# An attention kernel whose written-out engine order begins earlier, with another load order

## The chip, the cores and the metric

The kernel runs on one core of one Trainium2 chip. Its five engines run their own instruction queues in order and meet only through semaphores: TensorE (PE, matrix products into PSUM), VectorE (DVE), ScalarE (ACT), GpSimd (POOL) and SyncE (SP, which here issues DMA transfers). The metric is the device time of one execution in microseconds (us), the median of the runs shown.

## The reference

There are 2048 tokens (S) of width 512 (D), 32 query heads of width 16 (Dh), one key head and one value head that all query heads share, and an MLP of inner width 1792. Cut to what is computed:

```
x  = A_x                                    # 2048 x 512, bfloat16
xn = (x - mean) / sqrt(var + 1e-5)          # layer norm over each token's 512
q  = xn @ wq  -> 32 heads x 16;  k = xn @ wk;  v = xn @ wv        # one k, one v
p  = softmax(q k^T / 4)                     # 32 heads x 2048 x 2048, no mask
s  = concat_heads(p v) @ wo
g  = silu( silu(xn @ w1) @ w2 )
out = x + s * g
```

## The kernel before

**Tiles.** Tokens are cut in 16 tiles of 128 and in 4 chunks of 512 (four tiles each). A chunk serves twice, as 512 queries and as four key tiles. The heads are taken in four octets; of an octet the four even heads make one group and the four odd heads the next, so there are 4 chunks x 4 octets x 2 = 32 head groups. In a head group, the score block of one head with one key tile is a slot (128 keys x 512 queries): 32 x 4 heads x 16 key tiles = 2048 slots.

**PE's two modes.** A score matmul (L1068) uses 32 rows of the array, one head in each strip of 32 rows. Up to four of them, with different strips and each with its own PSUM bank, run side by side: a *score group*. A group that holds a second, *late* score for a strip in use is a *double group*. All else goes by *rounds*, four matmuls side by side that each fill 32 columns: PV (probabilities times values, L1494), the products h (with w1), z (with w2), q and w (with wo) at L696, and the keys K (L743). A *column run* is the rounds between two score groups. Tokens are turned (features to partitions) by PE transposes, eight to a pair of tiles (L712); values V are small matmuls at L773. A round of a product may instead be cut into four *gap pieces* (L808), each of which goes in a row strip that a score group leaves unused. There are seven PSUM banks for scores and products, and bank 7 gathers the PV output of one head group.

**Two ways to an exponential.** An *A slot* is read from PSUM by ACT, which writes exp to `pa_sb` (L1941, one, two or three banks in one instruction) and gives one PV matmul. A *D slot* is evicted by DVE as integers (`db_sb`, L1204, *score eviction*) that read as bfloat16 are a rough exp; POOL adds three constants to them, four slots at a time (int64 add into `ds_sb`, L1414, *shift*), and the four versions are PV matmuls with differently weighted values, whose sum is a better exp. Four D slots so cost four evictions, three shifts and 16 PV matmuls. DVE can do a shift too, but does none here. After a head group DVE transposes the PV output and divides by the softmax's sum (steps a to d, L1550 on).

**The other work on DVE and ACT.** Norms on DVE: statistics of a tile (L607), their aggregate (L611), eight small *root steps* for 1/sqrt, a chain, for four tiles at once (L625 to L634), and the normalised tile (L639). For chunk 0 ACT takes part. The turned tokens of a pair of tiles are copied from PSUM by DVE (L725). Keys are evicted at L757 and values at L782, queries at L818. Silu takes a tanh on ACT (L860, `t_sb`) and a product on DVE (L862, the *gate*). Keys for the odd heads lie 16 partitions further: a DMA that POOL issues copies them (`kt_sb`, L1573, *key copy*), once per chunk. While there are no other instructions, PE multiplies zeros (`zer_sb`): in full width ahead of the first tokens (L1878), in half width by rounds later (the *zero fills*, at L696 by the shared helper `col4`).

**Memory.** The D path's shift buffers `ds_sb` number eight; the last four hold the four chunks of x until their tiles are normalised. Loads go through SP's queue: four single tiles of chunk 0, the small weights and wq, then chunks 1, 2 and 3 of x, then w1 (1.75 MB), w2 (1.75 MB) and wo.

**What sets the order.** Class `Planner` lays out all instructions before the program is built: `place` puts an instruction at the end of an engine's list, `add` hands in a `Task` with a priority and a gate, and `best` picks for an engine the ready task of the lowest priority number. The main loop advances the engine whose planned clock is lowest. The prologue's jobs (turns T, keys K and values V of chunks 0 to 3, `NPRO` of them) and everything around them are placed by such rules: `pe_step` for PE, `act_step`, `generic_step`. From a certain state on the strings in `ORDER` dictate what each engine takes next:

```
at["on"] = st["pro"] >= NPRO and not active and x_free[0] and not any(pl.tasks[e] for e in (AC, DV, PO)) and (
    pl.clk[PE] <= min(pl.clk[e] for e in (AC, DV, PO)))
```

So in the kernel before the table begins when keys, values and turns of all four chunks are done. In PE's string, `S21+4B.` is a score group of two A and one D slot (the codes give bank, head group and strip; the last character is a gap piece's strip or a dot), `L` a late score, `Paads-` a PV round with the kind of each strip (a: from `pa_sb`, d: `db_sb`, s: `ds_sb`), `N5` starts the next job in bank 5, `J` is one more round of the active job. ACT's string has the banks per exp and T for a tanh, DVE's string digits (score eviction of that bank) and H (gate), Q (queries), a to d, V and W (outputs), POOL's string only 0 (the first shift in waiting). When the strings end, the rules take over again: last halves of PV, output products with wo of the last chunk, their sums with x, and stores.

Two rules hold before the table: `want_d` allows D slots only when the keys of all 16 tiles have been evicted, and shift buffers 4 to 7 come free together, when all 16 tiles are normalised (`check_x_free`, `make_shifts`).

## Time and profile before

| | |
|---|---|
| median of 3 runs | 657.98 us (657.75 to 658.15) |
| the profiled execution's own time | 658.13 us |
| its span in the trace | 656.3 us |
| granted TensorE clock | 1.00 |
| PE busy | 646.6 us (99%), 9007 matmuls |
| ACT busy | 642.2 us (98%), 748 instructions |
| DVE busy | 614.7 us (94%), 1094 |
| POOL busy | 585.0 us (89%), 583 |
| DMA | 12.86 MB, 20 GB/s on average |
| largest groups | shifts 577.0 us (567), exp 604.4 us (651), score evictions 481.3 us (756) |

The span is what the profiler saw of one execution; the device time lies a little above. Busy is the time in which at least one of an engine's instructions runs. PE's matmuls overlap, four of a group or round run side by side, and their ends are modelled, so the sums of PE's groups exceed its busy time and a busy PE need not be PE at its best; what one step of PE costs is read from the start of one to the start of the next. In rows of the order of time the columns are the start, the time from the first start to the last end of the instructions in the row, engine, line, operation, output and inputs, shape, and the count of like instructions in a row, with a bracket where the engine stood idle before it: for how long, and what released it. In rows of groups, "busy, mean" is followed by the idle time ahead of the group and the engine that ended most of it.

### The profile page before, as it was taken

The page shows a single profiled execution, that of the slowest core. Times are in us where ns is not written, and L with a number is a line of the kernel's source. Part 1 is how long each engine was busy: PE and PEld are TensorE (multiplying, and loading weights), DVE is VectorE, ACT ScalarE, POOL GpSimd, SP SyncE. Part 2 cuts the span into 40 slices and gives each one's busy share as a digit, 9 for nine tenths or more (in the row PEclk, how much of TensorE's full clock was granted, in tenths as well). Part 3 has the DMA queues.
Part 4 walks back from the last instruction along what each step waited for, and adds up shares of the span by engine and source line. Part 5 has one row for each costly group of instructions (what it writes and reads, how often), then busy time and mean ns, then how long its engine had stood idle before and what let it go on. Part 6 is the DMA issues. An engine that isn't in the chain of part 4 may idle for free.

```text
span 656.3 us, 21267 instructions
## 1 busy us (share of the span) xinstructions
PE 646.6 (99%) x9007; PEld 199.4 (30%) x9007; DVE 614.7 (94%) x1094; ACT 642.2 (98%) x748; POOL 585.0 (89%) x583
## 2 busy tenths in 40 slices
...
PEclk9999999999999999999999999999999999999999
...
DMA packets 11501, 12.86 MB, mean 20 GB/s; under 512 B 1808, under 2 KB 10768, under 8 KB 11408
## 3 DMA queue, kind: packets, MB, share of 16 engines
...
q0 software_dynamic: 192, 0.46, 0.2%
q10 hardware_dynamic: 432, 0.39, 0.2%
q14 instruction: 21, 0.17, 0.1%
...
## 4 chain that ended last, share of the span: by engine, by line
PE 92%; POOL 3%; DVE 3%; DMA 1%; ACT 1%; SPq 0%; issue 0%; DVEq 0%
PE ps L1494 42%; PE ps L1068 30%; PE ps L696 19%; POOL ds_sb L1414 3%; DMA ds_sb<-in_A_x_dram 1%; DVE stats_sb L607 1%; ACT pa_sb L1941 1%; PE ps L712 0%; SPq L542 0%; DVE xn_sb L639 0%; DVE kt_sb L757 0%; DVE u_sb L862 0%; DVE xnT_sb L725 0%; DVE v_sb L782 0%; PE ps L743 0%
## 5 line engine op out<-in xcount | busy, mean ns | idle before, releaser
L1414 POOL INT64_ADD ds_sb<-db_sb x567 | 577.0, 1040 | 33.9 <-DVE otr_sb L1554 19.0
L1941 ACT ACTIVATE pa_sb<-ps 128x1024 bf16<-128x1024 f32 (+2 forms) x651 | 604.4, 1040 | 2.7 <-PE ps L1068 2.2
L1204 DVE TENSOR_SCALAR db_sb<-ps 128x512 uint16<-128x512 f32 x756 | 481.3, 682 | 23.4 <-PE ps L1068 12.7
L1494 PE MATMUL ps<-ds_sb,v_sb 128*32 128x512 bf16 x2268 | 287.8, 383 | 0.0
L1068 PE MATMUL ps<-qt_sb,kt_sb 32*128 32x512 bf16 x2048 | 246.1, 384 | 3.4 <-ACT pa_sb L1941 1.3
L1494 PE MATMUL ps<-pa_sb,v_sb 128*32 128x512 bf16 x1296 | 246.4, 383 | 0.0
L1494 PE MATMUL ps<-db_sb,v_sb 128*32 128x512 bf16 x756 | 185.6, 383 | 0.0
L1068 PEld LDWEIGHTS ps<-qt_sb,kt_sb 32*128 32x128 bf16 x2048 | 64.3, 90 | 252.5 <-ACT pa_sb L1941 155.4
L1494 PEld LDWEIGHTS ps<-ds_sb,v_sb 128*32 128x32 bf16 x2268 | 71.6, 95 | 68.4 <-issue 48.9
L1494 PEld LDWEIGHTS ps<-pa_sb,v_sb 128*32 128x32 bf16 x1296 | 60.6, 95 | 38.7 <-issue 28.1
L696 PE MATMUL ps<-xnT_sb,w_sb 128*32 128x512 bf16 x876 | 62.9, 382 | 0.0
L696 PE MATMUL ps<-w_sb,u_sb 128*32 128x512 bf16 x796 | 60.4, 383 | 0.0
L1494 PEld LDWEIGHTS ps<-db_sb,v_sb 128*32 128x32 bf16 x756 | 45.9, 95 | 22.8 <-issue 15.2
L860 ACT ACTIVATE t_sb<-ps 128x512 bf16<-128x512 f32 x72 | 44.8, 622 | 1.7 <-PE ps L696 1.7
L862 DVE SCALAR_TENSOR_TENSOR u_sb<-t_sb,ps 128x512 bf16<-128x512 bf16 x56 | 38.0, 678 | 1.3 <-ACT t_sb L860 0.9
L808 PE MATMUL ps<-w_sb,u_sb 32*128 32x512 bf16 x100 | 38.5, 384 | 0.0
L696 PEld LDWEIGHTS ps<-xnT_sb,w_sb 128*32 128x32 bf16 x876 | 19.1, 95 | 23.4 <-DVE db_sb L1204 6.0
L1573 POOL DMA_DIRECT2D kt_sb<-kt_sb x4 | 2.3, 566 | 24.7 <-DVE kt_sb L757 14.7
L696 PEld LDWEIGHTS ps<-w_sb,u_sb 128*32 128x32 bf16 x796 | 15.7, 95 | 22.2 <-issue 15.0
L1550 DVE STREAM_TRANSPOSE f_sb<-ps 128x512 f32<-128x512 f32 x31 | 21.9, 707 | 0.2
L696 PE MATMUL ps<-wo_sb,on_sb 128*32 128x512 bf16 x256 | 18.6, 382 | 0.0
L696 PE MATMUL ps<-xnT_sb,wq_sb 128*32 128x512 bf16 x228 | 17.0, 382 | 0.0
...
## 6 DMA issues: line engine op xcount, KB each, us to landing
...
xr_sb<-in_A_x_dram SPq DMA_DIRECT2D x16, 128.0 KB, 2.3
out_dram<-ob_sb SPq DMA_DIRECT2D x15, 128.0 KB, 1.7
...
ds_sb<-in_A_x_dram SPq DMA_DIRECT2D x2, 128.0 KB, 2.7
```

The lines of the kernel that those rows point to most:

```text
L607: ts_ = pl.add(Task(DV, 593.0, lambda v, t=t: v.bn_stats(stats_sb[:, t, :], x_tile(t)), [xkey(t)], [("st", t)], 1 + j, gate=(lambda j=j: S ...
L696: last = h.matmul(bank(b)[32 * j:32 * (j + 1), 0:n], lhsT=lhs(j), rhs=rhs, start=start, stop=stop, tile_position=(0, 32 * j), skip_group_c ...
L808: return (lambda pe: pe.matmul(bank(b), lhsT=lhs(k, rows, 0, P), rhs=rhs(k, rows), start=False, stop=last, tile_position=(32 * i, 0), skip ...
L860: t1 = Task(AC, 490.0, lambda a: a.activation(t_sb[:, k, :], src, ACT.Tanh, scale=scale), [held], [("t", k)], 0, [t0])
L862: t2 = Task(DV, T_P, lambda v: v.scalar_tensor_tensor(out=dst, in0=t_sb[:, k, :], scalar=1.0, in1=src, op0=ALU.add, op1=ALU.mult), [held, ...
L1068: return pe.matmul(bank(b), lhsT=kt_sb[32 * i:32 * i + 32, g % 2, kt * P:(kt + 1) * P], rhs=qt_sb[32 * i:32 * i + 32, (g // 2) % NQR, :], ...
L1204: bt.P[i] = pl.add(Task(DV, T_P, lambda v: v.tensor_scalar(db_sb[:, bt.b, i * NQ:(i + 1) * NQ], bank(b), 128.0 * LOG2E, 128.0 * (SHIFT_BET ...
L1414: whole["po"].append(pl.add(Task(PO, T_P64, lambda g, cols=cols: g.int64_add(ds_sb[:, s, cols].bitcast(U64), db_sb[:, bt.b, cols].bitcast( ...
L1494: h = pe.matmul(bank(OB)[32 * i:32 * (i + 1), cols], lhsT=lhs, rhs=rhs, start=s0, stop=s1, tile_position=(0, 32 * i), skip_group_check=True)
L1550: t1 = pl.add(Task(DV, T_TR, lambda v: v.transpose(f_sb[:, k, :], bank(OB)), [("ps", OB)], [("F", k)], 1, [norm.get(("m", g - 2))]))
L1573: kt1[c] = pl.add(Task(PO, T_SWDGE, lambda e: e.dma_start(kt_sb[DH:P, 1, cols], kt_sb[0:P - DH, 0, cols]), [("kt0", k) for k in range(4 * ...
L1941: op = pl.place(AC, 0.8333 * NQ * n + T_AF, lambda a: a.activation(pa_sb[:, s * NQ:(s + n) * NQ].rearrange("p (b n) -> p b n", n=NQ), ps3[ ...
```

## The change

- `ORDER` begins earlier: after the prologue jobs of chunk 0 (`N0` of them) have started, the first octet's queries and the keys of chunk 0 are placed and no job but V of chunk 0 is active. All four strings are new. The turns, keys and values of chunks 1 to 3 stand in PE's string as prologue jobs (`M` starts one; `J`, `K`, `L` are rounds of the first, second and third active job). The norms of chunks 1 to 3 stand in DVE's string: s statistics, g aggregate, r root step, x normalised tile, C turned-token copy, E keys, v values; h is a shift done by DVE. In POOL's string 0 is a shift, k a key copy, and y a point up to which POOL waits, in the plan, for one more DVE instruction that the code marks `ports=2`.
- `want_d` asks for four key tiles (`D_TILES`) in place of 16, and a shift buffer that holds a chunk of x comes free when that chunk's four tiles are normalised.
- Loads: chunk 1, first half of w1 (inner columns 0 to 895), chunk 2, chunk 3, second half of w1, w2, wo. The h products wait for their half of w1 alone.
- `keep_warm` puts half-width zero products in the planned gaps of PE within a window of the plan; they replace the zero fills of that stretch, for PE's rules no longer decide there.
- `turn` (tokens turned by DMA transposes) and the normalised tile on POOL exist in the code, but with `T_DMA = 4` and `XN_PO = 4` all 16 tiles are turned by PE and normalised by DVE.
- In the planner, a key copy's landing, loads' durations, and priorities of the norms have other values, and `finish` now marks an output product as done also when its last part was a gap piece.

The strings differ from the old ones all along, up to the last PV. In the changed file the lines lie lower: L747 products and fills, L763 turns, K L802, V L833, gap pieces L869, scores L1134, PV L1563, score evictions L1273, shifts L1484 (POOL) and L1477 (DVE), exp L2011, tanh L921, gate L923, statistics L625, normalised tile L663, turned-token copies L776, key evictions L816, queries L879, key copies L1642.

```diff
@@ -19,6 +19,9 @@
+WARM_END, START_US = 45000.0, 10.0
+T_KT1, X_KB, W1_KB = 3300.0, 700, 1200
+XN_PO, T_DMA, T_XN, D_TILES, AHEAD_PA = 4, 4, 1200.0, 4, 14
...
     PE: (
-        "S216CM.LdfPaaaaN0JS11Yu.LaNJJPaaaaS214Al.LdyPaddaS21N[,.PdaaaPssadS214Bk.N6JJJS21M[..PaassS21:Dm.PssssPssaaPa-ssS01-.S21"
...
+        "JS31Xgt+.JN2JJJS30+4M.N4JJJN5S30+Br.JS207M.PaaadJM0S20Bv.JS209R.LaGM4N0JJJS408Ely.PaaaaM3JJJM0S308E_.S40;Dkx.JM4PaaaaM1S"
+        "30Cfs.PaaaaN0JJS21CLZ.JS306gu.M4JJJPaadaS30*@M.M1JS21hu(.PaaaaS21@NY.M1M0S11is.LaXPaaaaS305BO.PddaaM0JJJS21Yhr.PasasPsss"
...
     AC: (
-        "1122222T22222T2T222221T2T22222222222T2T12222222322T221T222222T2T2222222322222222222222T22323232222222222222T222222212222"
...
+        "33T21111111T13T222122122121222113222222222T222T212222222222T2T3222T2T22T232222222222222T2T2T2232222221T122222222222T2311"
...
     DV: (
-        "356Q56050H506a262bHc6H54656156H1H45645645645646a6H1H5Q25265265b6c5d252H5465H6256256a5Hb6cH2623623635625625625656a56b5c6d"
...
+        "gsg0gvrrrrrrrrHxxxxssssggggQrCrHrCrrrrHrssssxxxxggggErvrCrCr4rQrrrxxxxEv04CC6E62363v62323252H5a264H16456456456456b5c5H65"
+        "H6232a3H5Hb1c4H1d236Q32632632632632636Ha6H6H3b2c32562626126H2652626a4b6c46d46H6154Q636326526524a343b4c343H34040630630630"
...
     PO: (
-        "000000000000000000000000000000000000000000000000000000000000000000000000000000000000000000000000000000000000000000000000"
...
+        "kkkyyyyyyyyyyyy000k0000000000000000000y000000000y00000000000000000000y00000000000000y0000000000000000000y000000000000000"
...
-        for j in range(1, 4):
+        H1 = P * (NFT // 2)
+        w1v = B_w1.rearrange("(dc p) f -> p dc f", p=P)
+
+        def load_x(j):
             dma(SP, "x", ds_sb[:, XB + j, :].bitcast(BF16).rearrange("p (t d) -> p t d", d=D),
-                xv[:, 4 * j:4 * j + 4, :], 512, ds_keys(XB + j), prio=1)
-        dma(SP, "w1", w1_sb[:], B_w1.rearrange("(dc p) f -> p dc f", p=P), 1792, ["w1"], prio=2)
-        dma(SP, "w2", w2_sb[:], B_w2.rearrange("(ft p) n -> p ft n", p=P), 1792, ["w2"], prio=3)
-        dma(SP, "wo", wo_sb[:], A_wo.rearrange("(o p) n -> p o n", p=P), 512, ["wo"], prio=4)
+                xv[:, 4 * j:4 * j + 4, :], X_KB if j == 1 else 360, ds_keys(XB + j), prio=1)
+
+        def load_w1(h):
+            dma(SP, "w1", w1_sb[:, :, h * H1:(h + 1) * H1], w1v[:, :, h * H1:(h + 1) * H1], 600, [("w1", h)], prio=1)
+        load_x(1)
+        load_w1(0)
+        load_x(2)
+        load_x(3)
+        load_w1(1)
+        for name, dst, src, kb in (("w2", w2_sb[:], B_w2.rearrange("(ft p) n -> p ft n", p=P), 1792),
+                                   ("wo", wo_sb[:], A_wo.rearrange("(o p) n -> p o n", p=P), 512)):
+            dma(SP, name, dst, src, kb, [name], prio=4).gate = lambda: T_DMA >= NC or len(turned) == 4 * (NC - T_DMA)
...
                 ts_ = pl.add(Task(DV, 593.0, lambda v, t=t: v.bn_stats(stats_sb[:, t, :], x_tile(t)),
-                                  [xkey(t)], [("st", t)], 1 + j,
-                                  gate=(lambda j=j: STG(j, xn_task, evac_kt)) if j > 1 else
+                                  [xkey(t)], [("st", t)], 1 + j if j < 1 else 0,
+                                  gate=(lambda j=j: (rs_task[j - 1].op if j > 2 else xn_task[7].op) is not None) if j > 1 else
                                   (lambda: ("xnT", 3) in pl.lastw) if j > 0 else None))
-                pl.add(Task(DV, 66.0, lambda v, t=t: v.bn_aggr(mv_sb[:, t, :], stats_sb[:, t, :]),
-                            [("st", t)], [("mv", t)], 1 + j, [ts_]))
+                ts_.tag = "s"
+                ag = pl.add(Task(DV, 66.0, lambda v, t=t: v.bn_aggr(mv_sb[:, t, :], stats_sb[:, t, :]),
...
-                xn_task[i] = pl.add(Task(DV, 323.0, lambda v, i=i: v.tensor_scalar(
+                xn_task[i] = pl.add(Task(DV if g < XN_PO else PO, 323.0 if g < XN_PO else T_XN, lambda v, i=i: v.tensor_scalar(
                     xn_sb[:, i % 4, :], x_tile(i), mv_sb[:, i, 0:1], rstd_sb[:, i:i + 1],
                     op0=ALU.subtract, op1=ALU.mult),
-                    [xkey(i), ("rs", a), ("mv", i)], [("xn", i % 4)], 1 + g, [t], ports=2,
+                    [xkey(i), ("rs", a), ("mv", i)], [("xn", i % 4)], 1 + g if g < 1 else -1, [t], ports=2,
                     gate=lambda i=i: i < 4 or i - 4 in t_done))
+                xn_task[i].tag = "x"
...
+        def keep_warm(extra):
+            pe = list(pl.order[PE])
+            for k, a in enumerate(pe[:-8]):
+                if a.t0 > WARM_END or a.mode not in ("C", "S") or a.t0 < START_US * 1000.0:
+                    continue
+                room = pe[k + 1].t0 - a.end - (0.0 if pe[k + 1].mode == a.mode else SWITCH) - 40.0
+                n = int(room / (MM / 2))
+                c = next((j for j in range(k + 1, k + 5) if pe[j].fresh), None)
+                if n < 1 or c is None:
+                    continue
+                bs = [b for b, (_, ds) in pe[c].fresh.items() if all(pl.vis(d, PE) <= a.end for d in ds) and not any(
+                    b in o.banks for o in pe[k + 1:c])]
+                if not bs:
+                    continue
+                b = bs[0]
+                i, ds = pe[c].fresh[b]
+                if a.mode == "C":
+                    emit = lambda pe, b=b: col4(pe, b, lambda j: zer_sb[:, 32 * j:32 * (j + 1)], zer_sb[:, 0:NQ // 2], True, True, NQ // 2)
+                else:
+                    emit = lambda pe, b=b, r=slice(32 * i, 32 * i + 32): pe.matmul(
+                        bank(b)[:, 0:NQ // 2], lhsT=zer_sb[r, 0:P], rhs=zer_sb[r, 0:NQ // 2], start=True, stop=True, tile_position=(r.start, 0))
+                for _ in range(n):
+                    a = extra(PE, emit, ds, a)
...
+        def turn(t):
...
+            pl.add(Task(SP, 1200.0, lambda e: e.dma_start_transpose(out=xnT_sb[:, :, t * P:(t + 1) * P], in_=xn_sb[:, t % 4, :]),
+                        [("xn", t % 4)], [("xnT", t)], 1, [xn_task[t]], placed, dma=2))
...
-                    lambda k, rows: xnT_sb[rows, k, c * NQ:(c + 1) * NQ], lambda k: ["w1"] + xnT_keys(c))
+                    lambda k, rows: xnT_sb[rows, k, c * NQ:(c + 1) * NQ], lambda k: [("w1", ft // (NFT // 2))] + xnT_keys(c))
...
+        N0 = len(jobs)
         for c in range(1, NC):
-            mk_T([4 * c, 4 * c + 1])
-            mk_T([4 * c + 2, 4 * c + 3])
+            if c < T_DMA:
+                mk_T([4 * c, 4 * c + 1])
+                mk_T([4 * c + 2, 4 * c + 3])
+            else:
+                for t in range(4 * c, 4 * c + 4):
+                    turn(t)
             mk_K(c, 4 * c, 4 * c + 4)
...
-            if any(k not in evac_kt or evac_kt[k].op is None for k in range(NKT)):
+            if any(k not in evac_kt or evac_kt[k].op is None for k in range(D_TILES)):
...
-                    free = [k for k in range(NDS) if ds_busy[k] == 0 and (k < XB or x_free[0])]
+                    free = [k for k in range(NDS) if ds_busy[k] == 0 and (k < XB or all(xn_task[4 * (k - XB) + r].op is not None for r in range(4)))]
...
                 x_free[0] = True
-                make_shifts()
...
-        at = dict.fromkeys((PE, AC, DV, PO), 0) if ORDER else None
+        at = dict.fromkeys((PE, AC, DV, PO, "n", "two"), 0) if ORDER else None
+
+        def started():
+            return st["pro"] >= N0 and all(t is not None and t.op is not None for t in (q_done.get(0), evac_kt.get(3))) and all(
+                jb.kind == "V" for jb in active)
 
         def ordered():
             if not at.get("on"):
-                at["on"] = st["pro"] >= NPRO and not active and x_free[0] and not any(pl.tasks[e] for e in (AC, DV, PO)) and (
-                    pl.clk[PE] <= min(pl.clk[e] for e in (AC, DV, PO)))
+                at["on"] = started() and pl.clk[PE] <= min(pl.clk[e] for e in (AC, DV, PO))
             return at["on"]
 
...
-            if c == "N":
-                jb, b = jobs[st["job"]], int(next_of(PE, 2)[1])
-                if b not in pool_free or jb.gate is not None and not jb.gate() or any(k not in pl.lastw for k in jb.rounds[0][1]):
+            if c in "NM":
+                jb, b = jobs[st["job" if c == "N" else "pro"]], int(next_of(PE, 2)[1])
+                if b not in pool_free or any(p.op is None for p in jb.preds) or jb.gate is not None and not jb.gate() or any(
+                        k not in pl.lastw for k in jb.rounds[0][1]):
                     return INF
-                st["job"] += 1
+                st["job" if c == "N" else "pro"] += 1
                 pool_free.remove(b)
                 jb.bank = b
                 active.append(jb)
                 at[PE] += 1
-            jb = next(jb for jb in active if jb.left and jb.pos < jb.end - (1 if jb.got else 0))
+            else:
+                jb = [jb for jb in active if jb.left and jb.pos < jb.end - (1 if jb.got else 0)]["JKL".index(c)]
             if any(k not in pl.lastw for k in jb.rounds[jb.pos][1]):
-                assert c != "N"
+                assert c not in "NM"
                 return INF
             at[PE] += 1
             do_job(max(pl.clk[PE], pl.ready(PE, jb.rounds[jb.pos][1], [("ps", jb.bank)] if jb.pos == 0 else ())), jb)
...
-            task = next((x for x in pl.tasks[e] if x.tag == tag), None)
+            task = next((x for x in pl.tasks[e] if x.tag == tag and (tag != "h" or pl.avail(x) is not None)), None)
...
+            if e == PO and c == "y":
+                if at["n"] >= at["two"]:
+                    return INF
+                at["n"] += 1
+                at[e] += 1
+                return True
+            if e == PO and c.isdigit():
+                ts = [x for x in pl.tasks[PO] if x.tag is None]
+                if len(ts) <= int(c) or pl.avail(ts[int(c)], False) is None:
                     return INF
                 at[e] += 1
-                pl.place_task(pl.tasks[PO][int(c)])
+                pl.place_task(ts[int(c)])
```

261 lines of the change are left out of this document (141 added, 120 removed).

## The prediction

> **What bounds the kernel now.** I read the page's first two parts, then busy time by stretch, the waits of TensorE (PE) and VectorE (DVE), and the order of time for prices.
>
> ```profile
> span 656.3 us, 21267 instructions
> PE 646.6 (99%) x9007; PEld 199.4 (30%) x9007; DVE 614.7 (94%) x1094; ACT 642.2 (98%) x748; POOL 585.0 (89%) x583
> PEclk9999999999999999999999999999999999999999
> ```
> ```profile
> 8.90:36.60 27.70, 24.39 (x417) 11.36 (x405) 25.39 (x77) 25.72 (x37) 2.77 (x5) 1.00 0.60 207
> 36.60:60.00 23.40, 23.33 (x313) 7.43 (x313) 22.75 (x39) 23.40 (x31) 19.09 (x19) 1.00 0.02 6
> 60.00:640.00 580.00, 579.15 (x8003) 171.64 (x7995) 552.56 (x930) 579.03 (x658) 550.63 (x542) 1.00 0.03 8
> 10.00:20.00 10.00, 8.24 (x146) 4.15 (x146) 9.65 (x34) 8.88 (x9) 0.68 (x1) 1.00 1.06 380
> ```
> Columns of the second fence: stretch, its length, then busy time and count of PE, weight load, DVE, ScalarE (ACT), POOL, the granted clock, DMA share, GB/s. From 60 to 640 us PE and ACT are busy throughout; DVE and POOL have some 5% left. Up to 36.6 us POOL does almost nothing, while DVE is busy 25.39 of 27.70 us. In the waits (total, times, longest) PE stood 0.7 us from 60 to 640, its only such row, and DVE waited 1.4 us for PE once in the first stretch:
>
> ```profile
> PE ps L1068 <- DVE u_sb L862: 0.7, 1, 0.7
> DVE kt_sb L757 <- PE ps L743: 1.4, 1, 1.4
> ```
> So PE's own work sets the middle, and the start is a race of DVE, ACT and PE. Prices of PE, from start to start:
>
> ```profile
> 42.02 0.39 PE L1068 MATMUL ps<-qt_sb,kt_sb 32*128 32x512 bf16 x3
> 42.35 0.39 PE L1494 MATMUL ps<-pa_sb,v_sb 128*32 128x512 bf16 x2
> 42.68 0.39 PE L1068 MATMUL ps<-qt_sb,kt_sb 32*128 32x512 bf16 x3
> ...
> 643.45 3.19 PE L696 MATMUL ps<-w_sb,u_sb 128*32 128x512 bf16 x56
> 646.47 1.04 PE L1494 MATMUL ps<-ds_sb,v_sb 128*32 128x512 bf16 x16
> ```
> A score group takes 0.33, a column run of one round 0.33, and 14 rounds of z 3.02. So: 0.325 a group, 0.216 a round, and 0.115 for each turn back from column to score mode.
>
> **The change, part by part: PE's work.** The two programs' instruction orders can be counted from the first score group to the last output product.
>
> ```
>                    groups (double)  column runs  rounds  turns and V   sum
> before, all        616 (4)          613          1630.0  5.3 us        629.0
> after,  all        613 (4)          608          1629.0  5.3 us        627.2
> before, to K of 3   15               13            32.5  4.8            18.2
> after,  to K of 3   17 (1)           14            36.0  4.7            19.8
> ```
> (0.325, 0.216 for the second half of a double group, 0.115, 0.216.) "K of 3" is the key projection of the last chunk. The rounds leave out zero fills: 60 matmuls of half width before (1.6 us), 12 after (0.3). The fall of 1.8 us has 12 PV matmuls less in it (0.65): 4 slots go from DVE to ACT, 752 of 756 stay, and 8 gap pieces of 132 become two rounds, which puts back 0.4.
>
> ```profile
> 9.94 0.39 PE L1068 MATMUL ps<-qt_sb,kt_sb 32*128 32x512 bf16 x3
> 33.74 1.04 PE L743 MATMUL ps<-xnT_sb,wke_sb 128*32 128x512 bf16 x16
> 36.17 0.39 PE L1068 MATMUL ps<-qt_sb,kt_sb 32*128 32x512 bf16 x3 [0.58 <-DVE u_sb L862]
> 651.34 0.39 PE L1754 MATMUL ps<-xr_sb,ident 128*128 128x512 bf16 x1
> ```
> The profiled run needs 23.8 us from 9.94 to the K of 3 for 18.2 us of work: 5.6 lost, 1.6 of them as fills. From there 33.74 + (629.0 - 18.2) = 644.5, and output products end at 651.34: 6.8 lost later, 0.58 of it in the wait at 36.17.
>
> **When the changed kernel reaches that place.** Its PE has 9.94 + 19.8 + 0.3 = 30.0 us at the earliest. But the K of 3 needs the turned tokens of chunk 3, which come last in a queue of DVE work. Prices:
>
> ```profile
> 14.93 1.28 DVE L607 BATCH_NORM_STATS2 stats_sb<-ds_sb 128x6 f32<-128x512 bf16 x2
> 16.13 1.27 DVE L725 COPY xnT_sb<-ps 128x1024 bf16<-128x1024 bf16 x2
> 27.79 0.46 DVE L782 TENSOR_TENSOR v_sb<-ps,wj_sb 128x320 bf16<-128x320 f32 x1
> 28.17 0.16 DVE L625 TENSOR_SCALAR var_sb<-mv_sb 128x4 f32<-128x4 f32 x1
> 28.57 0.16 DVE L631 SCALAR_TENSOR_TENSOR var_sb<-rstd_sb 128x4 f32<-128x4 f32 x1
> 28.77 0.16 DVE L633 TENSOR_TENSOR var_sb<-var_sb 128x4 f32<-128x4 f32 x1
> 29.16 0.16 DVE L631 SCALAR_TENSOR_TENSOR var_sb<-rstd_sb 128x4 f32<-128x4 f32 x1
> 29.24 0.68 DVE L818 TENSOR_SCALAR qt_sb<-ps 128x512 bf16<-128x512 f32 x1
> 30.23 1.38 DVE L639 TENSOR_SCALAR xn_sb<-ds_sb,mv_sb,rstd_sb 128x512 bf16<-128x512 bf16 x4
> 31.52 0.68 DVE L862 SCALAR_TENSOR_TENSOR u_sb<-t_sb,ps 128x512 bf16<-128x512 bf16 x1
> 32.12 1.28 DVE L725 COPY xnT_sb<-ps 128x1024 bf16<-128x1024 bf16 x2
> 36.61 2.54 DVE L1204 TENSOR_SCALAR db_sb<-ps 128x512 uint16<-128x512 f32 x4
> 39.06 0.68 DVE L818 TENSOR_SCALAR qt_sb<-ps 128x512 bf16<-128x512 f32 x1
> 3.23 5.65 DMA ds_sb<-in_A_x_dram
> ```
> One statistic 0.60, one turned-token copy 0.595, values 0.38, a root step 0.20 in a chain and 0.08 when a long operation fills the latency, one normalised tile 0.32, one eviction 0.61. Chunk 1 has landed at 8.88, in the same queue position. From there to the last turned-token copy the changed DVE order has 12 statistics (7.2), 12 aggregates at 0.08 (1.0), 24 root steps, of which 13 still chained (3.5, against 4.8 unmixed), 12 tiles (3.9), 6 copies (3.6), 3 values (1.2), and evictions: 2 K, 2 q, 3 gates, 4 score (6.7). That is 27.1, so 36.0 us. Before, these copies start at 32.12 and the K of 3 at 33.74, with 2 K, 1 q, 2 gates and no score eviction in front. So the changed kernel starts the K of 3 later by 2.3 us and has done more: 55 score matmuls against 45, one q more. Of 36.0 - 9.94, 6.0 us are lost plus 0.3 of fills, 0.7 more than before. Bounds: PE's own 30.0 below; 37.8 above, if DVE meets as many waits as before (0.4 + 1.4). I take 36.0: the row of 1.4 us waited for this very K projection, behind which long work now stands.
>
> **The other parts.** First half of w1 ahead of chunks 2 and 3: 0.92 MB more ahead of them, at 380 to 207 GB/s (the rows above) 2.4 to 4.4 us, so it lands at 11.3 to 13.3, and the first gate rounds, which stand at 11.2 in PE's count, hold PE by 0.1 to 2.1. Behind them wait score groups; ACT has six exps of the first two groups to do meanwhile. This lies under the 6 us for which PE waits for DVE anyway; without that cover it costs up to 2.1. Chunk 2 lands at 12.7 to 15.8, and DVE reaches it at 16; w2 and wo land as late as now, and nothing reads them early. SP issues one DMA more, before anybody waits for SP. One of POOL's key copies moves behind three shifts.
>
> ```profile
> L1573 POOL DMA_DIRECT2D kt_sb<-kt_sb x4: 527/527/683, 10.8 to 35.8; - x4
> ...
> DMA to landing us min/median/max: 2.1/3.7/6.2
> ```
> The first copy of keys to the odd heads, issued at 10.8, took the longest, 6.2 us, so until 17.0 with loads in flight; the changed PE has a score group on it from 15.5. That is 1.5 us, under the same cover: PE next stops at the K of 1, at 21.5 by the same sum up to the copies of chunk 1.
>
> ACT: the exp forms go from 559, 39, 53 to 539, 53, 56 (two, three, one bank):
>
> ```profile
> L1941 ACT ACTIVATE pa_sb<-ps 128x1024 bf16<-128x1024 f32 x559 | 529.1, 1051 | 1.1 <-PE ps L1068 0.9
> L1941 ACT ACTIVATE pa_sb<-ps 128x1536 bf16<-128x1536 f32 x39 | 57.1, 1473 | 0.1
> L1941 ACT ACTIVATE pa_sb<-ps 128x512 bf16<-128x512 f32 x53 | 30.1, 611 | 1.5 <-PE ps L1068 1.4
> ```
> -21.0 + 20.6 + 1.8 = +1.4 us at these durations, which overlap. I put it at nothing, since PE is the one with the least idle time; if ACT is the bound it costs 1.4 (a rival). POOL does 558 shifts of 567 and DVE six: cover for later waits.
>
> **Later losses.** Of the 6.8 us, the 0.58 has no counterpart, for each half of the last values stands behind a score group. Ten score evictions stand before that last values eviction, at 40.1 by the prices, where the kernel before has done five by then; I put this at 0.7 of waits saved, between 0 and 2.5. At the end the z rounds stand before the last score group; the last PV then waits for three shifts in a row on DVE: 0.3, between 0 and 1. So 6.8 - 0.6 - 0.7 + 0.3 = 5.8; range 4 to 10, the upper end because every engine follows a new fixed order.
>
> **Sum.** 36.0 + (627.2 - 19.8) + 5.8 = 649.2 for the end of output products, against 651.34: -2.1. What follows (last half PV, 48 output matmuls, sums, stores) is the same code. The profiled execution took 658.13, span plus 1.8; the median of three is 657.98. I count from the median: 655.9.
>
> **Rivals.**
> *Given back.* DVE meets the waits of before (K of 3 at 37.8), the rest as above: 657.7, no change. For it: each engine keeps strict order, so a late gate input stalls the norms behind it. Against: the mixed root steps leave room.
> *ACT is the bound.* It has 1.4 us more work and at most 2.0 us of idle time to win before 36.6 (25.72 busy of 27.70): 657.4 to 659.4, nearest 657.8 with most of it won. For it: ACT is busy 579 of 580 us. Against: these durations overlap.
> *Later waits go.* The 6.8 us lost after the K of 3 are small hold-ups of PE by evictions, exps and shifts; if the score evictions done early and 9 shifts less on POOL halve what I keep of them (5.8 to 2.9): 653.0, at best 651.5. For it: POOL's 1.04 us a shift leave it some 5%; against: ACT's share does not fall.
> *Slower.* One mechanism: norms of chunks 2 and 3 now stand in DVE's queue behind gate, q and score evictions, each waiting for PE, which itself waits for turned tokens: a loop. Every us of DVE wait goes to the end. It decides from 3.4 us on (2.1 + 1.3); at 5 it gives 660.9. For it: before, norms had few evictions in front; against: three waits of 2.2 us in all there.
> *Clock.* The opening shows PE at half rate:
>
> ```profile
> 2.39 0.15 PEld L1878 LDWEIGHTS ps<-zer_sb 128*128 128x128 bf16 x1 [0.28 <-issue]
> 2.81 0.15 PEld L1878 LDWEIGHTS ps<-zer_sb 128*128 128x128 bf16 x1 [0.28 <-issue]
> 5.69 0.75 PEld L1878 LDWEIGHTS ps<-zer_sb 128*128 128x128 bf16 x4 [0.17 <-issue]
> ```
> Zero products follow one another by 0.42 us, and from about 5.4 on by 0.19: some 3.8 us at half rate, 1.9 us lost. Afterwards the granted clock is 1.00 in every stretch. Now fills go from 60 to 12, and PE may stand up to 2.2 us before the K of 1. If it drops to half rate once more for as long, 657.8; by the rows after 5.4 us, where PE pauses as at 36.17 (0.58), it does not. The Trainium skill ("TensorE: Matmul & The Clock Gate", Part 1: The HAM clock gate) says that an idle window of about 3.4 us halves the clock; by it a pause of 2.2 us would mostly not, and the sum stays.
>
> **How the numbers follow.** Mine 0.44 (654.2 to 656.6), later waits go 0.13, given back or ACT bound 0.22, loop 0.17, clock 0.04. A measurement can tell 0.2% (1.3 us) from nothing. Faster: 0.44 + 0.13 + 0.01 = 0.58; same 0.23; slower 0.19. The range 652.3 to 660.3 leaves out the ends of "later waits go" and of the loop.
>
> **What would show it.** Right: K of 3 between 35 and 37, DVE waits under 1 us from 9 to 36, PE 60 to 640 with as little waiting, first shift on POOL near 35, clock at 1.00. Wrong: a first gate round after 13, a DVE wait over 1.5 us in the norms, PE waits for POOL after 60, or a tail over 8 us from the last half PV (648.52 before, so 7.8).

## The result, and the profile after

The changed kernel takes 655.25 us (median of five executions, 654.86 to 656.04) against 657.98 (657.75 to 658.26): ratio 0.9958, interval 0.9947 to 0.9969, 2.7 us faster. The forecast was 655.9, range 652.3 to 660.3. The profiled execution took 654.86, with a span of 653.0 (before: 658.13 and 656.3). Of the five executions three had a granted clock of 0.999 or 1.000 and took 654.9 to 655.3, two had 0.997 and took 656.0; where a difference below is smaller than that, executions of equal clock are compared, named as such.

The first part of the page of the changed kernel, and its busy times by stretch (columns as in the prediction):

```profile
span 653.0 us, 21151 instructions
PE 643.4 (99%) x8946; PEld 197.9 (30%) x8946; DVE 615.2 (94%) x1096; ACT 642.6 (98%) x745; POOL 575.0 (88%) x574
```
```profile
8.90:36.60 27.70, 23.91 (x390) 10.80 (x378) 26.75 (x81) 26.15 (x37) 4.26 (x7) 1.00 0.62 204
36.60:60.00 23.40, 23.05 (x314) 7.04 (x315) 22.90 (x39) 23.40 (x28) 20.88 (x22) 1.00 0.02 7
60.00:640.00 580.00, 579.71 (x8043) 172.56 (x8043) 550.52 (x925) 579.96 (x659) 543.38 (x535) 1.00 0.03 8
```
Up to 36.6 us DVE is busy 26.75 of 27.70 us, 1.4 more than before. The middle looks as before: PE and ACT without a pause. POOL did 7.2 us less from 60 to 640, ACT 0.9 us more. The order of time of PE, with the marks of the prediction:

```profile
10.24 0.39 PE L1134 MATMUL ps<-qt_sb,kt_sb 32*128 32x512 bf16 x3
12.18 1.05 PE L747 MATMUL ps<-xnT_sb,w_sb 128*32 128x512 bf16 x16 [0.64 <-ACT pa_sb L2011]
17.71 0.39 PE L1134 MATMUL ps<-qt_sb,kt_sb 32*128 32x512 bf16 x2 [0.65 <-DMA kt_sb<-kt_sb]
21.67 1.04 PE L802 MATMUL ps<-xnT_sb,wke_sb 128*32 128x512 bf16 x16
24.47 0.40 PE L1134 MATMUL ps<-qt_sb,kt_sb 32*128 32x512 bf16 x4 [1.16 <-ACT pa_sb L2011]
25.62 0.62 PE L763 MATMUL ps<-ident,xn_sb 128*128 128x128 bf16 x8 [0.47 <-DVE xn_sb L663]
35.56 1.05 PE L802 MATMUL ps<-xnT_sb,wke_sb 128*32 128x512 bf16 x16
...
643.87 1.02 PE L1563 MATMUL ps<-ds_sb,v_sb 128*32 128x512 bf16 x12
645.49 0.28 PE L1563 MATMUL ps<-pa_sb,v_sb 128*32 128x256 bf16 x3
645.59 2.84 PE L747 MATMUL ps<-wo_sb,on_sb 128*32 128x512 bf16 x48
648.36 0.39 PE L1824 MATMUL ps<-xr_sb,ident 128*128 128x512 bf16 x1
```
The first score group starts at 10.24 (9.94 before), the first gate rounds at 12.18, the K of 3 at 35.56 (33.74 before; 36.0 forecast), and the output products end at 648.36 (651.34 before; 649.2 forecast). From the last half PV at 645.49 to the end of the span it is 7.5 us. From the K of 3 on the counted work is 607.4, so 648.36 - 35.56 - 607.4 = 5.4 us were lost later (5.8 forecast; this term is what is left over, not a measured wait). As a sum the prediction holds in each of its terms. The experiments show that the sum was not the cause.

The turned-token copies of chunk 3, which the prediction put last in a queue of DVE work, in DVE's order of time:

```profile
34.22 1.29 DVE L776 COPY xnT_sb<-ps 128x1024 bf16<-128x1024 bf16 x2
```
They end at 35.51, just ahead of the K of 3.

The end of the span, PE's last score group and ACT's rows, before and after:

```profile
642.25 0.40 PE L1068 MATMUL ps<-qt_sb,kt_sb 32*128 32x512 bf16 x4
642.87 2.11 ACT L1918 ACTIVATE pa_sb<-ps 128x512 bf16<-128x512 f32 x4
646.70 0.60 ACT L860 ACTIVATE t_sb<-ps 128x512 bf16<-128x512 f32 x1 [1.72 <-PE ps L696]
```
```profile
641.80 0.39 PE L1134 MATMUL ps<-qt_sb,kt_sb 32*128 32x512 bf16 x3
642.89 1.70 ACT L1988 ACTIVATE pa_sb<-ps 128x512 bf16<-128x512 f32 x4
647.37 0.60 ACT L973 ACTIVATE xn_sb<-ps 128x512 bf16<-128x512 f32 x1 [2.78 <-PE ps L747]
```
ACT's last exp ends at 644.98 before and at 644.59 after, 0.4 us apart, while the spans differ by 3.3. So 2.9 us of the difference lie behind the last exp: 11.3 us before, 8.4 after. From the start of the last score group it is 14.1 us before and 11.2 after. Before, the 14 rounds of the last z product (643.45, 3.02 us) stand behind that group: the first half of them runs beside the last exps, and the PV rounds that could have run there come after them. After, the 14 rounds stand in front, the first and the last of them at

```profile
629.51 1.04 PE L747 MATMUL ps<-w_sb,u_sb 128*32 128x512 bf16 x16
638.33 0.38 PE L869 MATMUL ps<-w_sb,u_sb 32*128 32x512 bf16 x1
```

### The profile page after: what moved, and what is told of

Same layout as the page of the kernel before. It is cut to its first block, busy times and chain, and to the rows that moved or that the text cites. A ratio compares the mean times of both kernels' runs of the same rounds, so it can differ in the third digit from the quotient of the medians.

```text
span 653.0 us, 21151 instructions
## 1 busy us (share of the span) xinstructions
PE 643.4 (99%) x8946; PEld 197.9 (30%) x8946; DVE 615.2 (94%) x1096; ACT 642.6 (98%) x745; POOL 575.0 (88%) x574
## 4 chain that ended last, share of the span: by engine, by line
PE 94%; DVE 3%; ACT 2%; issue 0%; DVEq 0%
PE ps L1563 43%; PE ps L1134 30%; PE ps L747 20%; ACT pa_sb L2011 2%; DVE stats_sb L625 1%; PE ps L1948 1%; PE ps L763 0%; DVE xnT_sb L776 0%; DVE xn_sb L663 0%; DVE u_sb L923 0%; DVE db_sb L1273 0%; DVE mv_sb L630 0%; ACT xn_sb L973 0%; DVE var_sb L656 0%; DVE var_sb L654 0%
## 5 line engine op out<-in xcount | busy, mean ns | idle before, releaser
L2011 ACT ACTIVATE pa_sb<-ps 128x1024 bf16<-128x1024 f32 (+2 forms) x648 | 605.8, 1058 | 1.1 <-PE ps L1134 0.9
L1484 POOL INT64_ADD ds_sb<-db_sb x558 | 567.1, 1038 | 39.8 <-DVE otr_sb L1623 19.4
L1273 DVE TENSOR_SCALAR db_sb<-ps 128x512 uint16<-128x512 f32 x752 | 479.0, 683 | 25.8 <-PE ps L1134 14.5
L1563 PE MATMUL ps<-ds_sb,v_sb 128*32 128x512 bf16 x2256 | 285.8, 383 | 0.0
L1134 PE MATMUL ps<-qt_sb,kt_sb 32*128 32x512 bf16 x2048 | 244.6, 384 | 3.1 <-ACT pa_sb L2011 1.6
L1563 PE MATMUL ps<-pa_sb,v_sb 128*32 128x512 bf16 x1299 | 246.0, 383 | 0.0
L1563 PE MATMUL ps<-db_sb,v_sb 128*32 128x512 bf16 x752 | 186.4, 384 | 0.0
L1134 PEld LDWEIGHTS ps<-qt_sb,kt_sb 32*128 32x128 bf16 x2048 | 63.6, 91 | 250.3 <-ACT pa_sb L2011 145.5
L1563 PEld LDWEIGHTS ps<-ds_sb,v_sb 128*32 128x32 bf16 x2256 | 71.3, 95 | 64.0 <-issue 45.1
L1563 PEld LDWEIGHTS ps<-pa_sb,v_sb 128*32 128x32 bf16 x1299 | 60.4, 95 | 40.6 <-issue 29.9
L747 PE MATMUL ps<-xnT_sb,w_sb 128*32 128x512 bf16 x872 | 64.5, 382 | 0.7 <-ACT pa_sb L2011 0.6
L747 PE MATMUL ps<-w_sb,u_sb 128*32 128x512 bf16 x796 | 61.0, 383 | 0.0
L1563 PEld LDWEIGHTS ps<-db_sb,v_sb 128*32 128x32 bf16 x752 | 46.1, 94 | 24.3 <-issue 16.3
L921 ACT ACTIVATE t_sb<-ps 128x512 bf16<-128x512 f32 x72 | 45.5, 633 | 0.0
L923 DVE SCALAR_TENSOR_TENSOR u_sb<-t_sb,ps 128x512 bf16<-128x512 bf16 x56 | 38.0, 679 | 1.0 <-ACT t_sb L921 0.6
L869 PE MATMUL ps<-w_sb,u_sb 32*128 32x512 bf16 x100 | 38.4, 384 | 0.0
L747 PEld LDWEIGHTS ps<-xnT_sb,w_sb 128*32 128x32 bf16 x872 | 19.1, 95 | 24.7 <-issue 6.3
L1642 POOL DMA_DIRECT2D kt_sb<-kt_sb x4 | 2.3, 568 | 22.7 <-DVE var_sb L647 15.6
L747 PEld LDWEIGHTS ps<-w_sb,u_sb 128*32 128x32 bf16 x796 | 14.9, 95 | 22.9 <-issue 16.3
L747 PE MATMUL ps<-wo_sb,on_sb 128*32 128x512 bf16 x256 | 18.3, 382 | 0.0
L747 PE MATMUL ps<-xnT_sb,wq_sb 128*32 128x512 bf16 x240 | 16.7, 381 | 0.0
```

Of the source, the lines that this page charges most:

```text
L747: last = h.matmul(bank(b)[32 * j:32 * (j + 1), 0:n], lhsT=lhs(j), rhs=rhs, start=start, stop=stop, tile_position=(0, 32 * j), skip_group_c ...
L869: return (lambda pe: pe.matmul(bank(b), lhsT=lhs(k, rows, 0, P), rhs=rhs(k, rows), start=False, stop=last, tile_position=(32 * i, 0), skip ...
L921: t1 = Task(AC, 490.0, lambda a: a.activation(t_sb[:, k, :], src, ACT.Tanh, scale=scale), [held], [("t", k)], 0, [t0])
L923: t2 = Task(DV, T_P, lambda v: v.scalar_tensor_tensor(out=dst, in0=t_sb[:, k, :], scalar=1.0, in1=src, op0=ALU.add, op1=ALU.mult), [held, ...
L1134: return pe.matmul(bank(b), lhsT=kt_sb[32 * i:32 * i + 32, g % 2, kt * P:(kt + 1) * P], rhs=qt_sb[32 * i:32 * i + 32, (g // 2) % NQR, :], ...
L1273: bt.P[i] = pl.add(Task(DV, T_P, lambda v: v.tensor_scalar(db_sb[:, bt.b, i * NQ:(i + 1) * NQ], bank(b), 128.0 * LOG2E, 128.0 * (SHIFT_BET ...
```

## The experiments

All are edits of the changed kernel; the diffs are shortened and simplified to the lines that act, some with a comment added. "Equal clock" means executions with a granted clock of 0.999 or 1.000. The kernel before ran beside every experiment, with medians of 658.1 to 658.4 us against 657.98 beside the changed kernel. Times of different experiments are therefore comparable to some 0.3 us only; where that matters a second figure goes by the distance from the kernel before.

**The load order undone.**

```diff
         load_x(1)
-        load_w1(0)
         load_x(2)
         load_x(3)
+        load_w1(0)
         load_w1(1)
```

> The changed kernel with chunks 2 and 3 of x loaded ahead of both halves of w1, every engine's order unchanged. Theory (the opening is one chain on DVE in strict order, and each us of it goes to the end): the first half of w1 lands near 14.6 us instead of 11.17, the first gate rounds start near 14.7 instead of 12.18, the norms behind the first gate slip by as much, the K of 3 starts at 37.5 to 38.1 instead of 35.56, and the time is 2.0 to 2.5 us longer. Rival (loads hidden): the statistics find their data earlier and the gate's delay is absorbed; K of 3 within 0.5 of 35.56, time within 0.5 us. Rival (clock): the pause of some 3 us on PE halves the clock once, and 1 to 2 us come on top.

659.81 us (12 executions, 658.13 to 662.05), ratio to the kernel before 1.0028 (1.0018 to 1.0037): 4.6 us slower than the changed kernel. PE's order of time:

```profile
15.30 1.66 PE L747 MATMUL ps<-xnT_sb,w_sb 128*32 128x512 bf16 x16 [4.22 <-DMA w_sb<-in_B_w_dram]
39.66 1.05 PE L802 MATMUL ps<-xnT_sb,wke_sb 128*32 128x512 bf16 x16
```
PE stands 4.2 us for the first half of w1, so the gate rounds start 3.1 us later (12.18 in the changed kernel) and not 2.5 as expected. They take 1.66 us and not 1.05, for the clock falls behind that pause: it is 0.80 from 15 to 16 us and 0.50 from 16 to 19. The K of 3 starts 4.1 us later. No execution kept its clock (0.992 to 0.997); the shortest is 3.2 us above 654.9. The rival "hidden" falls; the chain and the clock rival hold together. In this order the early half of w1 is needed.

**The fills taken out.**

```diff
-WARM_END, START_US = 45000.0, 10.0
+WARM_END, START_US = 0.0, 10.0
```

> The changed kernel without its 12 zero products between 14 and 19 us; nothing else moves. Theory (fills lie in pauses and the clock stays): no change, within 0.3 us, executions alike. Rival (clock): in the five executions of the changed kernel the granted clock was 0.997 to 1.000, and the two at 0.997 took 656.0 against 654.9; without the fills more executions show 0.997 or less, each 1 us or more longer.

654.98 us (654.79 to 656.47), ratio 0.9953 (0.9940 to 0.9966). The 12 fills cost nothing. One execution stood at 0.997, 656.47, the rest took 654.8 to 655.2; against two of five that is too few to tell whether these fills change how often the clock falls. The profile is of the one at 0.997, and so shows where it happens, in PE's order of time and in the busy times by stretch:

```profile
24.58 0.39 PE L1134 MATMUL ps<-qt_sb,kt_sb 32*128 32x512 bf16 x4 [1.22 <-ACT pa_sb L2011]
25.77 0.62 PE L763 MATMUL ps<-ident,xn_sb 128*128 128x128 bf16 x8 [0.51 <-DVE xn_sb L663]
26.65 0.90 PE L763 MATMUL ps<-ident,xn_sb 128*128 128x128 bf16 x8
```
```profile
23.00:25.00 2.00, 0.78 (x13) 0.26 (x12) 2.00 (x5) 2.00 (x3) 0.00 (x0) 1.00 0.48 158
25.00:26.90 1.90, 1.39 (x24) 0.97 (x24) 1.90 (x10) 1.89 (x3) 0.00 (x0) 0.98 0.01 4
26.90:30.90 4.00, 4.00 (x36) 1.25 (x33) 2.63 (x9) 2.00 (x4) 0.53 (x1) 0.58 0.12 35
```
PE is busy 2.2 of 3.9 us from 23.0 to 26.9 (0.9 of them with transposes), its longest pause 1.22 us; then eight transposes take 0.90 instead of 0.62, and the clock stands at 0.58 on the mean of the next 4.0 us, which is 3.4 us at half.

**DVE's work of the opening cut.**

```diff
-v.bn_stats(stats_sb[:, t, :], x_tile(t))
+v.bn_stats(stats_sb[:, t, :], x_tile(t) if t < 12 else x_tile(t)[:, 0:16])
```

> The changed kernel with the statistics of chunk 3's four tiles taken over 16 columns instead of 512, so that the norm of chunk 3 is not the reference's; 2.1 us less DVE work at 22.5 to 24.9. Theory (DVE sets the opening): normalised tiles of chunk 2 and its turns 2 us earlier, K of 3 at 33.5 to 34.2, and the time falls by 1.4 to 2.1 us. Rival (ACT is the bound): PE waits at 24.47 for an exp, ACT is busy 26.15 of 27.70 us there and its work is unchanged; the time falls by less than 0.4 us, wherever the K of 3 goes.

654.87 us (654.62 to 654.90), ratio 0.9950 (0.9938 to 0.9962); all five of equal clock, against 654.9 of the changed kernel: nothing.

PE's order of time in this run:

```profile
21.79 1.04 PE L802 MATMUL ps<-xnT_sb,wke_sb 128*32 128x512 bf16 x16
24.75 0.39 PE L1134 MATMUL ps<-qt_sb,kt_sb 32*128 32x512 bf16 x4 [1.21 <-ACT pa_sb L2011]
25.29 0.61 PE L763 MATMUL ps<-ident,xn_sb 128*128 128x128 bf16 x8
35.61 1.05 PE L802 MATMUL ps<-xnT_sb,wke_sb 128*32 128x512 bf16 x16
```
2.1 us less for DVE, and the first turn of chunk 2 starts 0.3 us earlier, the K of 3 not at all. (This execution starts its first score group 0.3 us late, at 10.55; counted from there the K of 3 gains 0.3.) DVE's queue alone does not set this place.

**ACT's work of the opening cut, alone and with DVE's.**

```diff
+            w = 3 * NQ // 4 if 3 <= at[AC] <= 18 else NQ      # at[AC]: place in ACT's order
-                pa_sb[...], ps3[:, b0:b1 + 1:step, :], ACT.Exp),
+                pa_sb[...][:, :, 0:w], ps3[:, b0:b1 + 1:step, 0:w], ACT.Exp),
```

> The changed kernel with the exps in places 4 to 19 of ACT's order reading 384 of 512 columns of each bank (POOL fills the rest with ones before 7.5 us, so the softmax of these slots is not the reference's): 20 banks by 128 columns, about 2.1 us less ACT work between 13.8 and 24 us. Theory (ACT alone sets the opening, since 2.1 us less of DVE moved nothing): K of 3 at 33.5 to 34.2 instead of 35.56, time 1.4 to 2.1 us shorter. Rival (two chains of equal length, ACT's and DVE's): the turns of chunk 2 then wait for DVE's normalised tiles (0.47 at 25.62 already), K of 3 at 35.0 to 35.5, time 0 to 0.5 us shorter.

> Both cuts: the shortened exps of the opening and the shortened statistics of chunk 3. Theory (ACT alone): as with the exps alone, K of 3 at 33.5 to 34.2. Rival (two equal chains): only now K of 3 moves, to 33.5 to 34.2, and the time falls by 1.4 to 2.1 us. Third (PE's own 30.0 us plus the first landing of the key copies bound it): less than 0.5 us even now.

656.83 us (10 executions, 655.42 to 657.77), ratio 0.9971 (0.9962 to 0.9980), and with both cuts 655.01 (654.94 to 656.18), 0.9954 (0.9941 to 0.9968). At equal clock that is 655.4 to 655.5 (four executions; the other six stood at 0.995 or 0.997) and 654.9 to 655.0: no gain in either. In both the K of 1 starts late, at 22.13 against 21.67, and with both cuts the first score group already does, at 10.90 against 10.24; the POOL instruction that was added may be the reason, which was not tested. So the place to compare is from there on, in PE's order of time of the run with both cuts:

```profile
22.13 1.04 PE L804 MATMUL ps<-xnT_sb,wke_sb 128*32 128x512 bf16 x16
24.79 0.39 PE L1136 MATMUL ps<-qt_sb,kt_sb 32*128 32x512 bf16 x4 [0.91 <-ACT pa_sb L2014]
35.74 1.05 PE L804 MATMUL ps<-xnT_sb,wke_sb 128*32 128x512 bf16 x16
```
The waits of the run with both cuts up to 36.6 us (total, times, longest):

```profile
PE ps L1136 <- ACT pa_sb L2014: 1.7, 4, 0.9
ACT pa_sb L2014 <- PE ps L1136: 1.8, 4, 0.8
```
From the K of 1 to the K of 3 it is 13.9 us in the changed kernel, 13.8 with DVE's cut (21.79 to 35.61) and 13.6 with both; from the first score group it is 25.3, 25.1 and 24.8. With both engines lighter PE still waits at 24.79 for an exp, and ACT waits 1.8 us for scores: each stands for the other. Two equal chains should have given 1.4 to 2.1 us; the third expectation (under 0.5 even now) is the nearest. The round trip of PE, exp, free bank and next group in the written order would explain it, but no run here isolates it.

**ACT's, then PE's work of the middle cut.**

```diff
+            w = NQ // 2 if at[AC] > 80 and at[AC] % 40 == 0 else NQ    # exps, columns read
...
+            if st["due"] and half is None and len(mm) == 4 and not any(x[3] or x[4] for x in mm):
+                cols = slice(0, NQ // 16)                               # one PV round in 48
```

> The changed kernel with some 16 two-bank exps between about 70 and 640 us, one in 40, that read half the columns (the rest of their probabilities is stale): 0.43 us each, 6.8 us less ACT work. Theory of the prediction (PE's own steps set the middle): time unchanged, within 0.5 us. Rival (ACT is the bound): the time falls by 2 to 6 us, as far as PE's slack lets it.

> The changed kernel with one PV round in 48 cut to 32 of 512 columns (its part of the sum is left out): some 31 rounds, 0.16 to 0.19 us each, 5.0 to 5.9 us less PE work, all other work as it is. Theory of the prediction (PE sets the middle): the time falls by 3 to 5.9 us. Rival (ACT is the bound): less than 1 us. If neither this nor the exps' cut alone moves the time, both engines are bound together, as the order table was balanced.

ACT's cut: 13 exps, of them 4 with three banks, 6.4 us by count; 655.63 us (654.91 to 656.60), ratio 0.9961 (0.9947 to 0.9974); at equal clock 654.9 and 655.1: nothing. PE's cut came to 21 rounds (84 short matmuls), 0.186 each, 3.9 us; 654.67 (654.07 to 655.38), ratio 0.9945 (0.9932 to 0.9959); at equal clock 654.1 and 654.2, so 0.75 us (1.0 by the distance from the kernel before): a fifth to a quarter of the price. Each of these figures rests on two executions. "PE's own work sets the middle" is refuted as a price for each step, and so is "ACT is the bound".

**Both cut in the same places.**

> The changed kernel with both cuts in the same places: 13 exps of half the columns (6.4 us less ACT work) and behind each of them two or three PV rounds of 32 columns (30 rounds, 5.6 us less PE work; neither result is the reference's). PE alone gave 0.75 us for 3.9 us less work, ACT alone nothing for 6.4. Theory (PE and ACT are locked to each other by seven banks and the written order): together 4 to 5.6 us shorter. Rival (a third engine, DVE or POOL, or fixed latencies hold the pace): not over 1.5 us shorter.

655.03 us (654.81 to 655.39), ratio 0.9949 (0.9936 to 0.9962). All four executions have a clock of 0.997; against the two of the changed kernel at 0.997 (656.0) that is 1.0 us (1.3 by the distance from the kernel before) for 5.6 us of PE and 6.4 of ACT.

**POOL cut as well**, with the nine fills described below:

```diff
+                if st.get("due2", 0) > 0:        # the next shift after each shortened exp
+                    st["due2"] -= 1
+                    pop.emit = lambda g: g.int64_add(ds_sb[:, s, 0:2 * NQ].bitcast(U64), db_sb[:, bt.b, 0:2 * NQ].bitcast(U64), words)
```

> The kernel with nine fills (654.84), and in 13 places between some 90 and 630 us three cuts: an exp of half the columns, two or three PV rounds of 32 columns behind it, and the next shift on POOL over half of its columns (0.5 us each, 6.6 us less POOL work; the rest of the shifted slots is stale). From 60 to 640 us POOL was busy 543.4 us of 580 and waited 27.6 us for DVE's otr and ob instructions, 6.5 us for scores and PE, so it has hardly more room than PE or ACT. Theory (POOL is the third engine in the lock): 3 to 6 us shorter than 654.84. Rival (DVE or fixed latencies hold the pace): about as with the two cuts, which gave some 1.1 us once 1.1 us for the halved clock in all four executions is taken off: 653.3 to 654.3.

653.21 us (652.97 to 653.44), ratio 0.9921 (0.9908 to 0.9935), all of equal clock: 1.6 us less than the nine fills alone, 0.3 to 0.6 more than with two cuts. The 13 shifts came to 0.43 us less each, 5.5 us in all. The middle by busy times, and the waits in it:

```profile
60.00:640.00 580.00, 576.58 (x8067) 172.54 (x8059) 550.72 (x927) 576.83 (x661) 538.82 (x536) 1.00 0.03 8
```
```profile
PE ps L1141 <- DVE db_sb L1280: 1.6, 7, 0.4
PE ps L1141 <- DVE qt_sb L886: 1.3, 4, 0.3
ACT pa_sb L2026 <- PE ps L1141: 2.5, 9, 0.6
DVE db_sb L1280 <- PE ps L1141: 14.2, 37, 1.3
```
With three engines lighter PE and ACT each stand some 3.1 us longer in the middle (576.6 and 576.8 busy against 579.7 and 580.0), and DVE, whose work was not cut, is as busy as it was. POOL is not the whole of it: PE's waits for DVE come to the same 1.6 and 1.3 us in the run with two cuts. These two rows are all but 0.2 us of what PE waits in the middle, and in each of these waits DVE is busy throughout, while ACT waits for PE's scores. So at the places of the cuts the traces point to DVE's evictions and queries as what comes next. That DVE holds the pace is not shown: no run cuts its work there, and over the middle it waits 14.2 us for PE.

**The last z product put back behind the last scores.**

```diff
-"...PaaaaN2JJJS31)7Xt.PddddPddssJPssdsPsssdS21gtO0PasssS20*71...JJJS21)4Z3JJS21gtO0JJPssaa..."
+"...PaaaaS31)7Xt.PddddPddssPssdsPsssdS21gtO.PasssS20*7....S21)4Z.S21gtO.Pssaa..."
```

> The changed kernel with the last z product (14 rounds, two of them as gap pieces) taken out of the last 25 us of the order and done behind the last score group, as in the kernel before; its tanh and gate go last on ACT and DVE. Theory of the prediction (PE's steps add up wherever they stand): the 14 rounds, 3.0 us, leave the one place and fill the other, time within 0.6 us. Rival (what counts is what stands behind the last exp, since ACT's last exp ended at 644.98 before and 644.59 after while the end moved by 3.3 us): ACT cannot use the room that the rounds leave, the last exp ends where it did, and the time is 2.4 to 3.0 us longer, which gives back nearly all of the gain.

659.65 us (12 executions, 657.85 to 661.40), ratio 1.0015 (1.0003 to 1.0026). Five executions of equal clock took 657.9 to 658.2, 3.0 us more than the changed kernel's 654.9 and 0.4 us less than the kernel before in the same comparison (658.36); by the distance from the kernel before the product's place is worth 2.6 us. Busy times of the changed kernel from 630 to 637 us, then those of this run by stretch, PE's order of time and ACT's, in an execution with a clock of 0.994:

```profile
630.00:637.00 7.00, 7.00 (x108) 2.10 (x100) 6.68 (x13) 7.00 (x10) 2.59 (x3) 1.00 0.00 0
```
```profile
630.00:637.00 7.00, 5.26 (x63) 1.46 (x55) 6.89 (x13) 7.00 (x12) 3.91 (x4) 1.00 0.01 2
637.00:641.00 4.00, 3.96 (x36) 0.88 (x37) 2.65 (x5) 3.38 (x4) 1.65 (x3) 0.57 0.00 0
```
```profile
644.10 0.39 PE L1134 MATMUL ps<-qt_sb,kt_sb 32*128 32x512 bf16 x3
646.16 3.20 PE L747 MATMUL ps<-w_sb,u_sb 128*32 128x512 bf16 x56
```
```profile
645.05 1.65 ACT L1988 ACTIVATE pa_sb<-ps 128x512 bf16<-128x512 f32 x4
649.41 0.60 ACT L921 ACTIVATE t_sb<-ps 128x512 bf16<-128x512 f32 x1 [2.71 <-PE ps L747]
```
In the changed kernel the 14 rounds stand between 629.5 and 638.7. In that stretch PE now is busy only 5.26 of 7.00 us and ACT still 7.00: ACT takes its exps no faster for the room. (DVE, at 6.89, has little room there either; no run cuts ACT or DVE in this stretch.) The last exp ends at 646.70 in this execution, whose clock fell in the opening and, after PE's new pauses, again after 637. Then z takes its 3 us as before: from the last score group to the end of the span it is 14.3 us, against 14.1 before and 11.2 in the changed kernel. The rival holds, put more exactly: what counts is what stands behind the last score group.

**Fills in the pauses that trip the clock.** Rounds of zeros added to the PV bank (start and stop false, so the sum stays as it is): six ahead of the score group at 24.47, and in the second run three more ahead of the turn at 25.62.

```diff
+            for g, n in MORE:                    # ((9, 6),) and ((9, 6), (10, 3))
+                a = groups[g]
+                for _ in range(n):
+                    a = extra(PE, lambda pe: col4(pe, OB, lambda j: zer_sb[:, 32 * j:32 * (j + 1)], zer_sb[:, 0:NQ // 2], False, False, NQ // 2), [], a)
```

> The changed kernel with six more half-width rounds of zero products, added to the PV bank, in PE's longest pause of the opening (1.16 us ahead of the score group at 24.47). Theory (clock plays no part): no change, within 0.2 us of the changed kernel, with the same two kinds of executions (654.9 and 656.0). Rival (clock): the executions at 0.997 are those in which this pause fell into one window of the clock gate; they disappear, and the median is 654.9.

> The changed kernel with nine half-width rounds of zeros added to the PV bank, six in the pause ahead of 24.47 and three in the one ahead of 25.62. Of 13 executions of kernels with the changed opening as it is, six showed a clock of 0.997 or less and took 1.1 to 1.5 us more; of five with the six fills none did. Theory (those pauses trip the clock gate): again no execution below 0.999, median 654.7 to 655.0. Rival (chance): two of five at 0.997, median as the changed kernel's 655.25.

654.85 us (654.47 to 655.20), ratio 0.9951 (0.9939 to 0.9963), and 654.84 (654.51 to 655.03), ratio 0.9945 (0.9933 to 0.9958). None of the ten executions is below 0.999. PE's order of time with nine fills:

```profile
22.82 0.39 PE L1141 MATMUL ps<-qt_sb,kt_sb 32*128 32x512 bf16 x3
23.14 0.84 PE L754 MATMUL ps<-zer_sb 128*32 128x256 bf16 x24
24.42 0.40 PE L1141 MATMUL ps<-qt_sb,kt_sb 32*128 32x512 bf16 x4 [0.45 <-ACT pa_sb L2018]
25.04 0.51 PE L754 MATMUL ps<-zer_sb 128*32 128x256 bf16 x12
25.62 0.62 PE L770 MATMUL ps<-ident,xn_sb 128*128 128x128 bf16 x8
```
The fills lie wholly in the pauses: the group at 24.42 and the turn at 25.62 start as they did (24.47 and 25.62). The triple cut above has the same nine fills and five more executions at 0.999 or 1.000, so none of 15 lost its clock. Of 17 executions whose opening is the changed kernel's as it is (its own five and those of the three cuts in the middle without fills; the run with z put back has a second place where its clock falls and is left out) ten did. If the fills did nothing and executions were independent, 15 in a row without would have a chance of (7/17)^15, practically none. Independent they may not be: all four executions with both middle cuts fell, and none of five with DVE's cut. But run side by side, four of four fell with both middle cuts and none of five with the nine fills. These are the best versions that keep the output: they remove the executions at 656, 0.4 us off the median, and leave the others where they were.

## Why the prediction was right, and where not

*The time*: 655.25 against 655.9, inside the likeliest case's own range (654.2 to 656.6).

*K of 3 at 36.0, a queue of DVE work worth 27.1 us*: 35.56. The queue is there as counted: DVE shows no wait in the opening, and its last copies end at 35.51. But as a reason it fails. With 2.1 us less in that queue the K of 3 starts at 35.61, and with ACT lighter as well it comes 0.3 us earlier, counted from the K of 1 (0.5 from the first score group). That the count of one engine came out is explained best by an order that keeps the engines nearly level there, so that each counts to the same place; that is argued, not shown.

*First half of w1, first gate rounds up to 2.1 us late, under cover*: w1's half landed in time, gate rounds at 12.18 with 0.64 us of waiting for an exp. Without the new load order they stand 4.2 us.

*First copy of keys late, 1.5 us under cover*: a wait of 0.65 us at 17.71, which fits the mechanism.

*Later losses 5.8*: 5.4. *Waits of PE from 60 to 640*: 0.29 us of idle against 0.85. DVE's longest wait up to 36 us was below 1 us and POOL's first shift starts at 34.4, as forecast; the tail from the last half PV is 7.5 us.

*PE's fall of 1.8 us in counted work, and the sum of -2.1*: this is the step that failed as a cause. "PE's own work sets the middle" priced each step at its full time. Cut from the middle, 3.9 us of steps were worth 0.75 to 1.0. The gain hangs on a place, not on a count: the 14 rounds of z that the prediction saw "before the last score group" and priced only by a later wait (0.3 us) are worth 2.6 to 3.0 us there. Ahead of the last score groups they lie wholly beside ACT's work; behind them only half of them do, and they push PV rounds behind the last exps. That the sum came out is luck in part. PE is busy to the end in both kernels, so its steps and losses add up to the span whatever moved them; but the forecast cut the later losses from 6.8 to 5.8 for other reasons, and with z put back the same sum would have had to lose some 8 us (an estimate: 5.4 and the 2.6 to 3.0). Shown is that the changed order without this move gains 0.4 us; that the move alone would do it in the old order was not tried.

*ACT is the bound (part of 0.22)*: wrong on the time (657.8), half right on the mechanism. ACT has 1.4 us more exp work (605.8 against 604.4), took it without loss, and by the busy times is what the stretch from 630 on runs by. Cutting its work in the middle gives nothing.

*The other rivals*: later waits did not go (5.4 us are left, not 2.9), and nothing was given back in the opening. The loop of DVE and PE did not close either; undoing the load order shows that a delay in the opening does go to the end, as that rival had it.

*The clock (0.04)*: too low. In two of five executions the clock was lower, and they took 1.1 us more; the run without fills shows one such fall. The forecast allowed 1.9 and a pause of 2.2 us ahead of the K of 1. Neither the place nor the pause was right: the clock fell after the K of 1 (21.67), around the turns that follow the pauses at 24.5 and 25.6. The 1.9 us went by the distance of the zero products in the opening; the trace's own clock reads 1.00 there. And the prediction argued from a single pause of 0.58 us after which the clock stayed. The Trainium skill ("TensorE: Matmul & The Clock Gate", Part 1: The HAM clock gate) speaks of an idle window of about 3.4 us that runs free of the kernel. That the clock falls in some executions only fits a free-running window, and the 3.4 us at half fit its length. But the window ahead of it was not idle: PE was busy 56% of the 3.9 us. On that point the measurement decides, with one thing open: 0.9 of these 2.2 busy us are transposes, and no run here shows whether the gate counts them as other work.
